# One fused attention and mixture-of-experts kernel: longer blocks of score and value matmuls, earlier q, k and v loads

## The chip, the cores and the metric

The kernel runs on one core of a Trainium2 chip. The metric is the device time of one execution in microseconds (us), lower is better. Three timed runs of the kernel before gave 984.13, 987.03 and 989.49 us; their median is 987.03 us. One more execution was taken with the hardware profiler: 983.65 us. In the instruction lists PE is TensorE's matmul stream, PEld its weight loads, DVE VectorE, ACT ScalarE, POOL GpSimd and SP SyncE, which issues most of the DMA transfers.

## What is computed

Attention with a sigmoid in place of a softmax, an expert layer with a capacity per expert, and a dense two-layer network, all in float32:

```
q, k, v: (4, 12, 448, 64)
scores = q @ k.T / 8 - log(448);  attn = sigmoid(scores);  x = attn @ v     -> (1792, 768)
logits = x @ w_gate (768, 8): tokens go to experts in the order of all logits, 224 per expert
out[mask_e] = relu(x[mask_e] @ w1[e] (768, 1024)) @ w2[e] (1024, 768)
h = relu(out @ w_in (768, 2048));  result = (s * h * h + b) @ w_out (2048, 768)
```

## The kernel before

The order of the instructions on each engine is the order of the source: nothing is rescheduled. The buffers of a tile pool are reused in turn, and an instruction that takes a buffer again waits for the last reader of its earlier content.

**Attention.** Heads are handled in 24 head pairs, i = 6 b + p (batch b of 4, pair p of 6). The q and k of a pair lie transposed as 128 x 448: head 0 in partitions 0 to 63, head 1 in 64 to 127. A score chunk c (112 of the 448 keys, both heads) is two calls of `T.matmul` with 64 rows and 112 columns of the array, one for each head (L236); a float32 call becomes two matmul instructions, so a chunk is 4 instructions and a pair has 16. A chunk fills one tile `psc` of two PSUM banks, and one ACT instruction (L237) turns it into `attn`. The value matmuls (L242) have 112 rows and 64 columns; again 16 instructions for a pair, all into one bank `pv`, which ACT copies to `xT` (L251).

`scores_av(n, i, mid)` (L222) weaves the scores of pair n = i + 1 with the values of pair i. Its loop over c2 emits two score chunks (8 instructions) and then two value chunks (8 instructions), twice. So TensorE goes score, value, score, value, 8 instructions in each block. PSUM has eight banks: two `psc` tiles (4), two `pv`, and one each for `plg` and `pt`.

**The gate.** `gate` (L253) multiplies finished pairs of xT with the gate weights, `gate_copy` has ACT copy the logits, `gate_turn` (L265) adds and transposes them, `prefs` (L278) is four DVE instructions on them. `mid(c)` (L357) places them inside the blocks: pairs 0 to 3 of a batch ahead of a score block at p = 5, pairs 4 and 5 between the two chunks of a score block at the next batch's p = 0, `gate_turn` at p = 1, and after it, at the end of that iteration, `prefs`. In the last batch `bracket` follows in three stages at p = 2, 3, 4 (DVE; PE L296 and DVE; PE L302 and DVE), and the gate of pairs 0 to 4, its copy and `gate_turn` stand around the two value blocks of the last pair. `gate_last` (L273) adds pair 5.

**Loads and conversions.** In iteration i SP issues `load_v(i + 2)` (4 buffers) and `load_qk(i + 3)` (4 buffers), 224 KB for each of v, k and q. The same SP queue carries `cv_in`, a load of 768 KB of 64-bit weights, and `cv_out`, a store of 384 KB: `convert` (L148) turns float64 into float32 bit patterns with four DVE instructions (L156 to L159), 1 or 2 conversions per iteration (`CONV`), 32 in all. The next `cv_in` waits until a conversion has read its buffer, and everything behind it in SP's queue waits with it. In the last iterations `w_dma`, `w_high` (ACT) and `w_low` (POOL) prepare the first expert weights.

After attention come the routing (rows of xT to DRAM, ten auction steps among PE, DVE and ACT), a gather, and the experts with the dense network.

Of the kernel before, what the change touches and what calls it, by code (L numbers as in the profile page):

```python
# [8 lines left out]
F32 = mybir.dt.float32  # L9
# [15 lines left out]
CP = 112  # L25
# [37 lines left out]
def tile_kernel(ctx, tc, qT, kT, v, wg, w1, w2, wi, wo, s2, b2, cst, out):  # L63
# [56 lines left out]
    qk = att.enter_context(tc.tile_pool(name="qk", bufs=4))  # L120
    vp = att.enter_context(tc.tile_pool(name="vp", bufs=2))
    at = att.enter_context(tc.tile_pool(name="at", bufs=2))
    ps_s = att.enter_context(tc.tile_pool(name="ps_s", bufs=2, space=PSUM))
    ps_v = att.enter_context(tc.tile_pool(name="ps_v", bufs=2, space=PSUM))
# [84 lines left out]
    def load_v(i):  # L209
        b, p = pairs[i]  # L210
        vt[i] = vp.tile([CP, NC, 128], F32, name="vt", bufs=4)
        nc.sync.dma_start(vt[i], v[b, p])
# [9 lines left out]
    def scores_av(n, i, mid):  # L222
        if n is not None:
            rq, rk = raw_qk.pop(n)
            attn[n] = at.tile([CP, 2, NC, S], F32, name="attn")
        if i is not None:
            a = attn.pop(i)
            pv = ps_v.tile([128, 512], F32, name="pv")
        for c2 in range(0, NC, 2):
            for c in (c2, c2 + 1):  # L230
                mid(c)
                if n is not None:
                    p = ps_s.tile([CP, 2, 512], F32, name="psc")
                    for j in range(2):
                        me = slice(j * D, (j + 1) * D)
                        T.matmul(p[:, j, :S], rk[me, c * CP:(c + 1) * CP], rq[me], start=True, stop=True)  # L236
                    A.activation(attn[n][:, :, c, :], p[:, :, :S], AF.Sigmoid, bias=nls[:CP],  # L237
                                 scale=1.0 / math.sqrt(D))
            for c in (c2, c2 + 1):
                if i is not None:  # L240
                    for j in range(2):
                        T.matmul(pv[j * 64:(j + 1) * 64, :S], vt[i][:, c, j * D:(j + 1) * D], a[:, j, c, :],  # L242
                                 start=(c == 0), stop=(c == NC - 1))
        if i is not None:
            b, p = pairs[i]
            xt = xT[:, p, b * S:(b + 1) * S]
            if i == len(pairs) - 1:
                A.copy(xt[:, :2 * CP], pv[:, :2 * CP])
                A.copy(xt[:, 2 * CP:], pv[:, 2 * CP:S])
            else:  # L250
                A.copy(xt, pv[:, :S])  # L251

    def gate(b, p0, p1, last):  # L253
        if p0 == 0:
            plg[b] = ps_l.tile([128, 512], F32, name="plg")
# [9 lines left out]
    def gate_turn(b, stop):  # L265
        lg = lgs.pop(b)
        pt = ps_l.tile([128, 512], F32, name="pt")
# [21 lines left out]
    def bracket(stage):  # L289
# [4 lines left out]
        elif stage == 1:  # L294
            pm = ps_l.tile([128, 512], F32, name="plg")
# [4 lines left out]
        else:  # L300
            pr = ps_l.tile([128, 512], F32, name="plg")
# [31 lines left out]
    cv_in()  # L333
    cv_in()
    cv_in()
    scores_av(0, None, lambda c: None)
# [14 lines left out]
    for i in range(N):  # L351
        b, p = pairs[i]
        if i + 2 < N:
            load_v(i + 2)
        if i + 3 < N:
            load_qk(i + 3)
        def mid(c):  # L357
            if b == B - 1 and p == 5:
                if c == 0:
                    gate(b, 0, 5, 5)  # L360
                elif c == 2:
                    gate_copy(b)
                elif c == 3:
                    gate_turn(b, False)
            elif p == 5 and c == 0:
                gate(b, 0, 4, 6)
            elif p == 0 and b and c == 1:
                gate(b - 1, 4, 6, 6)
            elif p == 0 and b and c == 3:
                gate_copy(b - 1)  # L370
            elif p == 1 and b and c == 0:
                gate_turn(b - 1, True)

        scores_av(i + 1 if i + 1 < N else None, i, mid)
        if p == 1 and b:
            prefs(b - 1)
# [442 lines left out]
```

## Time and profile before

| what | value |
|---|---|
| profiled execution | 983.65 us, its span 981.8 us |
| median of three timed runs | 987.03 us |
| PE busy | 938.5 us (96%) |
| DVE, ACT, POOL busy | 592.1, 449.7, 241.5 us |
| mean granted TensorE clock | 0.981 of full |
| PE matmul groups L236 and L242 | 86.1 and 82.8 us |
| DMA moved | 173.07 MB, mean 176 GB/s |

The span is counted from the first to the last instruction; 1.85 us of the profiled time lie around it. A merged row of the timeline gives the start, the time from the first start to the last end, engine, line, operation, the tile written and read, the shapes (rows*columns of the array, then the moving operand), the number of instructions, and in brackets the engine's idle time before it with what ended it. Matmul ends overlap the next start, so the pace of TensorE is read from differences of starts.

### The profile page before, as it was taken

What the parts mean: (1) busy time and instruction counts of PE and PEld (TensorE: products, weight loads), DVE (VectorE), ACT (ScalarE), POOL (GpSimd) and SP (SyncE); (2) the same over time, 40 slices, a digit from 0 to 9 for tenths busy, and PEclk for the clock granted to TensorE, in tenths of its full rate; (3) what the DMA queues carried; (4) which work ended last, traced back from release to release, by engine and by line L of the source; (5) the groups of instructions that cost most, each with busy time, mean ns of one, the idle gap of its engine ahead of it and who ended that gap; (6) DMA issues with size and microseconds to landing.
All of it is one profiled execution on the core that took longest, in us unless ns stands there. A gap on an engine that the chain in (4) does not pass through costs nothing.

```text
span 981.8 us, 13971 instructions
## 1 busy us (share of the span) xinstructions
PE 938.5 (96%) x5181; PEld 774.8 (79%) x5181; DVE 592.1 (60%) x984; ACT 449.7 (46%) x787; POOL 241.5 (25%) x183
## 2 busy tenths in 40 slices
PE   9999999768999999999999999999999999999997
PEld 3333333447889999988999999889999988899997
DVE  3655635774788970287777323877773288677320
ACT  5666657564654332366533223664332366533220
POOL 1000001225556565455200003551000164200001
PEclk9999999778999999999999999999999999999999
DMA  9999996373664344467443433664434476443321
GB/s 301 369 310 361 351 352 219 114 223 106 206 202 136 113 133 125 144 208 236 126 132 111 127 97 120 221 220 144 124 115 138 125 228 206 126 128 113 113 65 65
DMA packets 68455, 173.07 MB, mean 176 GB/s; under 512 B 7968, under 2 KB 24864, under 8 KB 68384
## 3 DMA queue, kind: packets, MB, share of 16 engines
q1 hardware_dynamic: 64256, 160.22, 50.8%
q0 software_dynamic: 2272, 11.01, 3.2%
q10 hardware_dynamic: 1856, 0.92, 0.3%
q8 instruction: 42, 0.69, 0.3%
q14 instruction: 29, 0.24, 0.1%
HBM read 148.52 MB, written 23.59 MB: 175 GB/s over the span
## 4 chain that ended last, share of the span: by engine, by line
PE 72%; DVE 16%; ACT 5%; issue 3%; DMA 2%; POOL 1%; POOLq 0%; ACTq 0%; SPq 0%; DVEq 0%
PE acc L690 8%; PE acc L691 8%; PE acc L692 8%; PE psc L236 8%; PE acc L741 8%; PE acc L742 8%; PE acc L743 8%; PE pv L242 8%; DVE u L652 6%; DVE wl L197 5%; PE acc L641 4%; ACT wh L186 2%; PE acc L642 2%; DVE tt L646 2%; DVE y L655 2%
## 5 line engine op out<-in xcount | busy, mean ns | idle before, releaser
L197 POOL TENSOR_TENSOR wl<-raw,wh 128x768 fp32r<-128x768 f32 (+1 forms) x89 | 196.5, 2215 | 422.2 <-ACT wh L186 404.5
L186 ACT CAST wh<-raw 128x768 fp32r<-128x768 f32 (+1 forms) x240 | 209.2, 879 | 160.2 <-PE acc L743 137.0
L197 DVE TENSOR_TENSOR wl<-raw,wh 128x768 fp32r<-128x768 f32 (+1 forms) x151 | 168.2, 1118 | 99.3 <-ACT wh L186 99.3
L741 PE MATMUL acc<-wh,gt 128*128 128x384 f32 x448 | 149.9, 335 | 0.0
L742 PE MATMUL acc<-wl,gt 128*128 128x384 f32 x448 | 149.7, 334 | 0.0
L743 PE MATMUL acc<-wh,gt 128*128 128x384 f32 x448 | 149.6, 334 | 0.0
L690 PE MATMUL acc<-y,wh 128*128 128x448 f32 x384 | 141.2, 368 | 0.0
L691 PE MATMUL acc<-y,wh 128*128 128x448 f32 x384 | 140.4, 366 | 0.0
L692 PE MATMUL acc<-y,wl 128*128 128x448 f32 x384 | 140.3, 365 | 0.0
L641 PE MATMUL acc<-u,wh 128*128 128x448 f32 x384 | 126.6, 384 | 14.2 <-DVE u L652 14.1
L641 PE MATMUL acc<-x,wh 128*128 128x448 f32 x384 | 124.2, 379 | 0.0
L237 ACT ACTIVATE attn<-psc,nls 112x896 f32<-112x896 f32 x96 | 92.1, 1005 | 54.3 <-PE psc L236 54.3
L642 PE MATMUL acc<-x,wl 128*128 128x224 f32 x384 | 102.3, 266 | 2.5 <-DVE wl L197 1.7
L642 PE MATMUL acc<-u,wl 128*128 128x224 f32 x384 | 102.9, 268 | 1.3 <-DVE wl L197 1.3
L714 ACT ACTIVATE r<-acc 128x448 f32<-128x448 f32 x64 | 34.9, 545 | 149.6 <-PE acc L692 149.6
L641 PEld LDWEIGHTS acc<-u,wh 128*128 128x128 f32 x384 | 72.8, 190 | 26.0 <-DVE u L652 20.8
L236 PE MATMUL psc<-rq,rk 64*112 64x448 f32 x384 | 86.1, 564 | 0.6 <-ACT attn L237 0.6
L742 PEld LDWEIGHTS acc<-wl,gt 128*128 128x128 f32 x448 | 84.1, 188 | 0.0
L741 PEld LDWEIGHTS acc<-wh,gt 128*128 128x128 f32 x448 | 84.1, 188 | 0.0
L743 PEld LDWEIGHTS acc<-wh,gt 128*128 128x128 f32 x448 | 84.1, 188 | 0.0
L242 PE MATMUL pv<-attn,vt 112*64 112x448 f32 x384 | 82.8, 552 | 0.0
L652 DVE SCALAR_TENSOR_TENSOR u<-tt,u 128x224 fp32r<-128x224 f32 x64 | 65.2, 1019 | 20.9 <-ACT u L651 19.1
(206 smaller groups left out, 1189.2 us busy)
## 6 DMA issues: line engine op xcount, KB each, us to landing
raw<-nw SPq DMA_DIRECT2D x128, 384.0 KB
raw<-in_w_dram SPq DMA_DIRECT2D x64, 384.0 KB
raw<-in_w_dram SPq DMA_DIRECT2D x48, 512.0 KB
craw<-in_wi_dram SPq DMA_DIRECT2D x16, 768.0 KB
nw<-co SPq DMA_DIRECT2D x32, 384.0 KB
craw<-in_wo_dram SPq DMA_DIRECT2D x16, 768.0 KB
rk<-in_kT_dram SPq DMA_DIRECT2D x24, 224.0 KB
rq<-in_qT_dram SPq DMA_DIRECT2D x24, 224.0 KB
```

Of the source, the lines that this page charges most:

```text
L186: A.copy(h[:, :k], raws[i][:, :k])
L197: eng.tensor_sub(lo[:, :k], r[:, :k], h[:, :k].bitcast(F32))
L236: T.matmul(p[:, j, :S], rk[me, c * CP:(c + 1) * CP], rq[me], start=True, stop=True)
L242: T.matmul(pv[j * 64:(j + 1) * 64, :S], vt[i][:, c, j * D:(j + 1) * D], a[:, j, c, :], start=(c == 0), stop=(c == NC - 1))
L641: T.matmul(p[:, :2 * CAP], wh[:, k], src[:, k].rearrange("p a s -> p (a s)"), start=(k == 0), stop=False)
L642: T.matmul(p[:, :CAP], wl[:, k], src[:, k, 0], start=False, stop=(k == n - 1))
L690: T.matmul(p, wh, src[:, k, 0], start=first, stop=False)
L691: T.matmul(p, wh, src[:, k, 1], start=False, stop=False)
L692: T.matmul(p, wl, src[:, k, 0], start=False, stop=last)
L741: T.matmul(ps[t][:, :DH], hi, wh[:, cols], start=(f == 0), stop=False)
L742: T.matmul(ps[t][:, :DH], hi, wl[:, cols], start=False, stop=False)
L743: T.matmul(ps[t][:, :DH], lo, wh[:, cols], start=False, stop=(f == KG - 1))
```

## The change

The weaving function is split in two. `scores(n, c0, c1)` emits score chunks c0 to c1 of pair n, `values(i)` all value matmuls of pair i and its copy. An iteration is now `values(i)` (16 instructions), `scores(i + 1, 2, NC)` and `scores(i + 2, 0, 2)` (16 together). Ahead of the loop all scores of pair 0 and half of those of pair 1 are made. `psc` gets three tiles of two banks, `pv` one bank, and the gate's tiles share one bank, `small`. The q and k of pair i + 4 (5 buffers) and then the v of pair i + 3 (5 buffers) are issued at the head of iteration i; pair 3's q and k and pair 2's v go ahead of the second `cv_in`. The gate's steps stand at the ends of iterations: pairs 0 to 3 (0 to 4 in the last batch) after p = 4, pairs 4 and 5 and the copy after p = 5, `gate_turn` and `prefs` after the next batch's p = 0, the stages of `bracket` after p = 1, 2, 3, and the last `gate_turn` after the loop.

```diff
@@ -117,11 +117,11 @@
     cgp = early.enter_context(tc.tile_pool(name="cgp", bufs=1))
 
     att = ExitStack()
-    qk = att.enter_context(tc.tile_pool(name="qk", bufs=4))
+    qk = att.enter_context(tc.tile_pool(name="qk", bufs=5))
     vp = att.enter_context(tc.tile_pool(name="vp", bufs=2))
     at = att.enter_context(tc.tile_pool(name="at", bufs=2))
-    ps_s = att.enter_context(tc.tile_pool(name="ps_s", bufs=2, space=PSUM))
-    ps_v = att.enter_context(tc.tile_pool(name="ps_v", bufs=2, space=PSUM))
+    ps_s = att.enter_context(tc.tile_pool(name="ps_s", bufs=3, space=PSUM))
+    ps_v = att.enter_context(tc.tile_pool(name="ps_v", bufs=1, space=PSUM))
     ps_l = att.enter_context(tc.tile_pool(name="ps_l", bufs=1, space=PSUM))
 
 
@@ -208,7 +208,7 @@
 
     def load_v(i):
         b, p = pairs[i]
-        vt[i] = vp.tile([CP, NC, 128], F32, name="vt", bufs=4)
+        vt[i] = vp.tile([CP, NC, 128], F32, name="vt", bufs=5)
         nc.sync.dma_start(vt[i], v[b, p])
 
     def load_qk(i):
@@ -219,40 +219,39 @@
         nc.sync.dma_start(rq, qT[b, p])
         raw_qk[i] = (rq, rk)
 
-    def scores_av(n, i, mid):
-        if n is not None:
-            rq, rk = raw_qk.pop(n)
+    def scores(n, c0, c1):
+        if n >= len(pairs):
+            return
+        if c0 == 0:
             attn[n] = at.tile([CP, 2, NC, S], F32, name="attn")
-        if i is not None:
-            a = attn.pop(i)
-            pv = ps_v.tile([128, 512], F32, name="pv")
-        for c2 in range(0, NC, 2):
-            for c in (c2, c2 + 1):
-                mid(c)
-                if n is not None:
-                    p = ps_s.tile([CP, 2, 512], F32, name="psc")
-                    for j in range(2):
-                        me = slice(j * D, (j + 1) * D)
-                        T.matmul(p[:, j, :S], rk[me, c * CP:(c + 1) * CP], rq[me], start=True, stop=True)
-                    A.activation(attn[n][:, :, c, :], p[:, :, :S], AF.Sigmoid, bias=nls[:CP],
-                                 scale=1.0 / math.sqrt(D))
-            for c in (c2, c2 + 1):
-                if i is not None:
-                    for j in range(2):
-                        T.matmul(pv[j * 64:(j + 1) * 64, :S], vt[i][:, c, j * D:(j + 1) * D], a[:, j, c, :],
-                                 start=(c == 0), stop=(c == NC - 1))
-        if i is not None:
-            b, p = pairs[i]
-            xt = xT[:, p, b * S:(b + 1) * S]
-            if i == len(pairs) - 1:
-                A.copy(xt[:, :2 * CP], pv[:, :2 * CP])
-                A.copy(xt[:, 2 * CP:], pv[:, 2 * CP:S])
-            else:
-                A.copy(xt, pv[:, :S])
+        rq, rk = raw_qk[n]
+        for c in range(c0, c1):
+            p = ps_s.tile([CP, 2, 512], F32, name="psc")
+            for j in range(2):
+                me = slice(j * D, (j + 1) * D)
+                T.matmul(p[:, j, :S], rk[me, c * CP:(c + 1) * CP], rq[me], start=True, stop=True)
+            A.activation(attn[n][:, :, c, :], p[:, :, :S], AF.Sigmoid, bias=nls[:CP], scale=1.0 / math.sqrt(D))
+        if c1 == NC:
+            raw_qk.pop(n)
+
+    def values(i):
+        a, v = attn.pop(i), vt.pop(i)
+        pv = ps_v.tile([128, 512], F32, name="pv")
+        for c in range(NC):
+            for j in range(2):
+                T.matmul(pv[j * 64:(j + 1) * 64, :S], v[:, c, j * D:(j + 1) * D], a[:, j, c, :],
+                         start=(c == 0), stop=(c == NC - 1))
+        b, p = pairs[i]
+        xt = xT[:, p, b * S:(b + 1) * S]
+        if i == len(pairs) - 1:
+            A.copy(xt[:, :2 * CP], pv[:, :2 * CP])
+            A.copy(xt[:, 2 * CP:], pv[:, 2 * CP:S])
+        else:
+            A.copy(xt, pv[:, :S])
 
     def gate(b, p0, p1, last):
         if p0 == 0:
-            plg[b] = ps_l.tile([128, 512], F32, name="plg")
+            plg[b] = ps_l.tile([128, 512], F32, name="small")
         for p in range(p0, p1):
             i = p % 4
             T.matmul(plg[b][i * 32:(i + 1) * 32, :S], wgs[:, p], xT[:, p, b * S:(b + 1) * S],
@@ -264,7 +263,7 @@
 
     def gate_turn(b, stop):
         lg = lgs.pop(b)
-        pt = ps_l.tile([128, 512], F32, name="pt")
+        pt = ps_l.tile([128, 512], F32, name="small")
         pts[b] = pt[:CP, :NC * E].rearrange("p (c e) -> p c e", e=E)
         for c in range(NC):
             T.matmul(pts[b][:, c], lg[:, c * CP:(c + 1) * CP], ct[:, C_SEL:C_SEL + E], start=(c == 0),
@@ -292,13 +291,13 @@
             V.tensor_reduce(mm[:CP, 0:1], lv, axis=AX.X, op=ALU.max)
             V.tensor_reduce(mm[:CP, 1:2], lv, axis=AX.X, op=ALU.min, negate=True)
         elif stage == 1:
-            pm = ps_l.tile([128, 512], F32, name="plg")
+            pm = ps_l.tile([128, 512], F32, name="small")
             T.transpose(pm[:2, :CP], mm[:CP], ident[:CP, :CP])
             m2 = ep.tile([2, 1], F32, name="m2")
             V.tensor_reduce(m2, pm[:2, :CP], axis=AX.X, op=ALU.max)
             V.tensor_scalar(dg, ident[:2, :2], m2, None, op0=ALU.mult)
         else:
-            pr = ps_l.tile([128, 512], F32, name="plg")
+            pr = ps_l.tile([128, 512], F32, name="small")
             T.matmul(pr[:, :2], on[:2], dg, start=True, stop=True)
             V.tensor_copy(mm, pr[:, :2])
             lb = ep.tile([128, 1], BF16, name="lb")
@@ -331,9 +330,12 @@
     load_v(1)
     load_qk(2)
     cv_in()
+    load_qk(3)
+    load_v(2)
     cv_in()
     cv_in()
-    scores_av(0, None, lambda c: None)
+    scores(0, 0, NC)
+    scores(1, 0, 2)
     nc.sync.dma_start(sb2[:, 0:1], s2.partition_broadcast(128))
     nc.sync.dma_start(sb2[:, 1:2], b2.partition_broadcast(128))
     G.memset(on, 1.0)
@@ -350,32 +352,25 @@
     N = len(pairs)
     for i in range(N):
         b, p = pairs[i]
-        if i + 2 < N:
-            load_v(i + 2)
+        if i + 4 < N:
+            load_qk(i + 4)
         if i + 3 < N:
-            load_qk(i + 3)
-        def mid(c):
-            if b == B - 1 and p == 5:
-                if c == 0:
-                    gate(b, 0, 5, 5)
-                elif c == 2:
-                    gate_copy(b)
-                elif c == 3:
-                    gate_turn(b, False)
-            elif p == 5 and c == 0:
-                gate(b, 0, 4, 6)
-            elif p == 0 and b and c == 1:
-                gate(b - 1, 4, 6, 6)
-            elif p == 0 and b and c == 3:
-                gate_copy(b - 1)
-            elif p == 1 and b and c == 0:
-                gate_turn(b - 1, True)
-
-        scores_av(i + 1 if i + 1 < N else None, i, mid)
-        if p == 1 and b:
+            load_v(i + 3)
+        values(i)
+        scores(i + 1, 2, NC)
+        scores(i + 2, 0, 2)
+        if p == 0 and b:
+            gate_turn(b - 1, True)
             prefs(b - 1)
-        if b == B - 1 and 2 <= p <= 4:
-            bracket(p - 2)
+        elif p == 4:
+            gate(b, 0, 4 if b < B - 1 else 5, 6 if b < B - 1 else 5)
+            if b == B - 1:
+                gate_copy(b)
+        elif p == 5 and b < B - 1:
+            gate(b, 4, 6, 6)
+            gate_copy(b)
+        if b == B - 1 and 1 <= p <= 3:
+            bracket(p - 1)
         if N - 6 <= i < N - 2:
             w_dma()
         if i >= N - 4:
@@ -384,6 +379,7 @@
         if i < N - 1:
             for _ in range(CONV[i]):
                 convert()
+    gate_turn(B - 1, False)
     gate_last(B - 1)
     prefs(B - 1)
     cv_out(0)
```

## Rows read from the trace of the kernel before

**Rows 1.** Windows: busy us (instructions) by engine, granted clock, DMA share, GB/s.

```profile
0.00:172.00 172.00, 170.24 (x820) 57.84 (x822) 92.26 (x143) 107.30 (x125) 7.19 (x17) 1.00 0.94 323
...
181.00:230.00 49.00, 32.50 (x201) 24.84 (x201) 30.04 (x215) 27.63 (x93) 11.90 (x23) 0.70 0.56 160
```

**Rows 2.** Timeline, PE, five score and five value blocks, first and last.

```profile
59.73 1.76 PE L236 MATMUL psc<-rq,rk 64*112 64x448 f32 x8
61.42 1.72 PE L242 MATMUL pv<-attn,vt 112*64 112x448 f32 x8
...
76.46 1.76 PE L236 MATMUL psc<-rq,rk 64*112 64x448 f32 x8
```

**Rows 3.** Timeline, PEld, weight loads inside one score and one value block.

```profile
60.20 0.18 PEld L236 LDWEIGHTS psc<-rq,rk 64*112 64x112 f32 x2 [0.20 <-issue]
60.58 0.18 PEld L236 LDWEIGHTS psc<-rq,rk 64*112 64x112 f32 x2 [0.20 <-issue]
...
61.85 0.14 PEld L242 LDWEIGHTS pv<-attn,vt 112*64 112x64 f32 x2 [0.23 <-issue]
62.23 0.14 PEld L242 LDWEIGHTS pv<-attn,vt 112*64 112x64 f32 x2 [0.23 <-issue]
```

**Rows 4.** Timeline, ACT, the two sigmoids of the block at 59.73.

```profile
60.85 1.91 ACT L237 ACTIVATE attn<-psc,nls 112x896 f32<-112x896 f32 x2 [1.35 <-PE psc L236]
```

**Rows 5.** Timeline, PE, a gate in the middle of a score block.

```profile
94.07 1.01 PE L236 MATMUL psc<-rq,rk 64*112 64x448 f32 x4
95.01 0.94 PE L258 MATMUL plg<-xT,wgs 128*32 128x448 f32 x4
95.89 1.01 PE L236 MATMUL psc<-rq,rk 64*112 64x448 f32 x4
96.83 1.72 PE L242 MATMUL pv<-attn,vt 112*64 112x448 f32 x8
```

**Rows 6.** Timeline, PE, scores of pairs 0 and 1, first values.

```profile
7.81 1.91 PE L236 MATMUL psc<-rq,rk 64*112 64x448 f32 x8 [0.36 <-ACT attn L237]
9.92 1.91 PE L236 MATMUL psc<-rq,rk 64*112 64x448 f32 x8 [0.21 <-ACT attn L237]
11.76 1.72 PE L242 MATMUL pv<-attn,vt 112*64 112x448 f32 x8
```

**Rows 7.** Timeline, PE, the last pairs of attention.

```profile
172.63 0.38 PE L302 MATMUL plg<-dg,on 2*128 2x2 f32 x2
173.78 1.69 PE L258 MATMUL plg<-xT,wgs 128*32 128x448 f32 x10 [0.77 <-DVE mm L303]
...
177.05 0.95 PE L270 MATMUL pt<-ct,lg 128*112 128x8 f32 x8
177.93 1.72 PE L242 MATMUL pv<-attn,vt 112*64 112x448 f32 x8
180.10 0.95 PE L275 MATMUL pt<-wgs,xT 128*112 128x8 f32 x8 [0.45 <-ACT xT L248]
```

**Rows 8.** Timeline, DVE, the last conversions and the last preferences.

```profile
168.39 2.46 DVE L159 CUSTOM_DVE_ANT_0 co<-co,cb__1306 128x1536 uint16<-128x1536 uint16 x1
...
176.16 0.55 DVE L156 TENSOR_SCALAR co<-craw 128x768 int32<-128x768 int32 x1
...
178.08 0.96 DVE L159 CUSTOM_DVE_ANT_0 co<-co,cb__1363 128x1536 uint16<-128x1536 uint16 x1
181.09 0.19 DVE L279 COPY L<-pt 112x32 f32<-112x32 f32 x1 [2.05 <-PE pt L275]
```

**Rows 9.** Timeline, POOL, beside them.

```profile
167.21 2.82 POOL L197 TENSOR_TENSOR wl<-raw,wh 128x768 fp32r<-128x768 f32 x1 [4.87 <-ACT wh L186]
```

**Rows 10.** Windows, as in Rows 1, a stretch without a hold of SP.

```profile
110.00:140.00 30.00, 30.00 (x150) 9.59 (x148) 16.80 (x24) 18.50 (x23) 0.00 (x0) 1.00 1.03 367
```

**Rows 11.** Timeline, SP and PE, issue and first use of pair 11's k.

```profile
66.68 0.46 SPq L217 DMA_DIRECT2D rk<-in_kT_dram  x1
...
79.80 1.39 PE L236 MATMUL psc<-rq,rk 64*112 64x448 f32 x6
```

## The prediction

> **What bounds the kernel now.** I read the windows first: in the first 172 us TensorE is busy for 170.24, at a granted clock of 1.00 of full (its 2.4 GHz level), while DVE and ACT are busy for 92 and 107 [rows 1]. So attention is bound by TensorE alone, and a microsecond saved there ends the stage a microsecond earlier. The DMA engines are busy for 94% of the same stretch [rows 1]; they are the next limit and have to be looked at. The routing behind it, 181 to 230 us, is a chain of short steps at a mean granted clock of 0.70 [rows 1] that the change doesn't touch.
>
> Then the timeline of TensorE. Five score and five value blocks of 8 follow each other from 59.73 to 76.46: 16.73 / 5 = 3.346 us for one of each, the score block 1.69 of it and the value block 1.66 [rows 2]. Inside a block the weight loads show the pace: the two matmuls of both heads run side by side, and the next two come 0.38 us later, in score blocks (60.20, 60.58) as in value blocks (61.85, 62.23) [rows 3]. Four such steps of 0.375 are 1.50 us. The rest, 0.19 for a score block and 0.155 for a value block, is paid once per block: when TensorE turns from 64 rows and 112 columns to 112 rows and 64 columns, or back, the next kind starts only after the last one has run out, and its first loads are not hidden. That is what longer blocks can save.
>
> **The change part by part, on TensorE.**
>
> *Blocks of 16.* From the first value matmul on, the kernel before runs 48 value blocks (two for each of 24 pairs) and 45 score blocks; the one after 24 and 23. Removed: 24 x 0.155 + 22 x 0.19 = 7.9 us. The matmuls stay the same in number. A block of 16 should take 8 x 0.375 + 0.19 = 3.19 us (scores) and 3.155 (values), an iteration 6.35 in place of 6.69.
>
> *The gate.* Pairs 4 and 5 of a batch stand in the middle of a score block: from 94.07 to 96.83 are 2.76 us, where the block alone takes 1.69, so 1.07 [rows 5]. At a block's edge the gate's own step is 0.88 (95.01 to 95.89), as it replaces one turn by two. Three batches x 0.19 = 0.6 us. The other gate steps stood at edges and stand at edges again: nothing.
>
> *The last batch.* The gate at 173.78 waited 0.77 us for DVE, which had just been asked to copy the result of the matmul at 172.63 [rows 7]. After, a whole iteration lies between them: 0.8 gained. `gate_turn` (177.05 to 177.93, 0.88) leaves the gap between the last two value blocks and goes behind them, where `gate_last` waits for the copies of xT anyway: the last block would have ended at 177.93 + 1.65 = 179.58 and `gate_last` began at 180.10 [rows 7], 0.52 later; now it begins 0.88 later. 0.88 - 0.36 = 0.5 gained.
>
> *Ahead of the loop.* Before, the third and the fifth score chunk waited 0.36 and 0.21 us for a sigmoid to free one of two psc tiles, and the first values began at 11.76 [rows 6]. With three tiles the sixth chunk waits for the third sigmoid. The first ended at 7.8 (it released the chunk at 7.81), two sigmoids take 1.91 us [rows 4], so the third ends at 9.7; the chunk takes 0.94 [rows 5], and the values begin at about 10.7: 1.0 gained, between 0 (ACT as before) and 1.2.
>
> Sum: 7.9 + 0.6 + 0.8 + 0.5 + 1.0 = 10.8 us.
>
> **What can wait in the new order.** An ACT iteration is four sigmoids (2 x 1.91) and a copy, 4.4 us of 6.35, so ACT keeps up. `pv` with one bank: its copy starts when the values are done, a score block of 3.19 us lies ahead of the next values; hidden. The sigmoids of pair i + 1's last two chunks are made in the first half of the score block and needed after it; hidden. One edge is sharp: the fourth chunk of a score block takes the psc tile of the first. Its sigmoid begins 1.12 us after the block (59.73 to 60.85) and ends about 1.0 later [rows 2, 4], at 2.1; the chunk is due at 0.46 + 5 x 0.375 = 2.34 (the first step is 0.46 long, 59.73 to 60.20 [rows 2, 3]), but its weights are loaded one step earlier, at 1.96. No such wait is in the trace. It costs nothing if the loads hide behind the step before, and at most 0.1 us x 22 if they don't, with nothing to gain from it: 0 to 2.2. I take 0.4, nearer the end at nothing, since the sigmoid ends before the matmul is due. Everything behind it on TensorE waits as well.
>
> The shared bank `small` is taken in turn by steps that are an iteration apart: nothing.
>
> **DMA and SP.** On SP's queue the loads of q and k pass those of v, and both come an iteration earlier in the order; the first conversions' loads come three transfers (0.7 MB, 2 us at 367 GB/s [rows 10]) later, and a conversion is not waited for. `prefs` now stands an iteration earlier in DVE's order while its matmul comes at nearly the same point of TensorE's, so DVE stands still longer there, and `cv_in` and the q, k and v loads behind it on SP wait with it. After the first hold, which ended with the gate's turn just ahead of 59.73, the k of pair 11 was issued at 66.68 and used at 79.80, 13.1 us later [rows 2, 11]. Now one conversion, some 4 us with its load, lies between the end of the hold and the next pair's q and k, and their use is two iterations and 4.75 us (a value block and half a score block) behind it: 2 x 6.35 + 4.75 - 4 = 13.4 us. The busiest batch carries 9 conversions (1.18 MB each) and six pairs (0.69 MB each), 14.7 MB in 6 x 6.35 + 3 x 0.88 (gate) = 40.7 us, 362 GB/s; 367 were moved from 110 to 140 us [rows 10]. Balanced, with the 13 us as a cushion: I cost it at nothing, and below as a rival.
>
> **DVE's last work.** Behind the matmul of the third `bracket` stage DVE now has three conversions ahead of the last `prefs` (it had one). Before: 172.63 to 176.16 for the stage, then 2.88 for a conversion (176.16 to 179.04), and then 2.05 us of waiting for TensorE [rows 7, 8]. After, DVE is done 3.53 + 3 x 2.88 = 12.2 us behind that matmul; TensorE needs 0.38 + 3.155 + 1.69 + 1.62 (173.78 to 175.40) + 3.155 + 0.88 + 0.99 (180.10 to 181.09 [rows 7, 8]) = 11.9. So this is a draw: the cover of 2 us is gone. One conversion lost 1.5 us (2.46 in place of 0.96 for its last step, 168.39) while POOL's subtraction ran from 167.21 to 170.03 [rows 8, 9]. With none such, DVE is early: 0; with two, late by 0.3 + 3.0 = 3.3. POOL has two subtractions in that stretch and may be the one that waits; I take 0.6, nearer the draw that the durations give. The Trainium skill ("SBUF — State Buffer", Who interferes with whom) says that a DVE instruction with two SBUF inputs and a reading GpSimd instruction shut each other out, and whoever issues first holds the port for its whole length; by that every meeting that POOL begins costs up to the 1.8 us of its subtraction, and two would make 3.6. The trace agrees in kind (1.5 us), and both lengthened here.
>
> Net: 10.8 - 0.4 - 0.6 = 9.8 us. The profiled execution took 983.65 us (981.8 of it span), so its counterpart is 973.9. The median of the runs shown, 987.03, lies 3.4 above it and the lowest at 984.13; from the median, **977.2 us**.
>
> **Rivals.**
> 1. *The end of attention is given to DVE, and the fourth chunk waits.* For it: the draw above. Against: each part has a way to cost nothing. With 3.3 and 2.2 the gain is 5.3 to 7: 981.
> 2. *The cost is paid per chunk, not per turn.* If a semaphore wait at each chunk made the first step long, blocks of 16 would save nothing: 10.8 - 7.9 = 2.9, less 1.0 as above: 985. Against it: a block holds two chunks, and the step between them is 0.38 like the others [rows 3].
> 3. *Loads of the value matmuls are not hidden in a long block.* Here a load of 0.14 us would be added to every step, and value blocks would keep their 0.155 per 8: 3.7 us less, 981. Rows 3 speak against it: 0.38 from step to step with the loads included. The Trainium skill ("TensorE: Matmul & The Clock Gate", What overlaps and what doesn't) says that weight loads overlap running matmuls only when their row groups differ, and the value matmuls use the same rows; the trace doesn't bear that out.
> 4. *Slower: the loads starve TensorE.* If the longer hold empties the DMA queues and the rate after it is not 367 but under 295 GB/s, a batch's 14.7 MB take 50 us in place of 40.7, more than the 6 or so of the cushion that a load's own 7 us leave. TensorE then stands still more than 3.3 us in each of three batches; at 5 us each the net is -15 + 10: 992 to 994. For it: 94% busy DMA and a mean of 323 GB/s [rows 1]. Against: that mean includes the holds, and without them 367 were reached [rows 10].
>
> **How the numbers follow.** Forecast 0.62, rival 1 0.17, rival 2 0.08, rival 3 0.06, rival 4 0.07. The forecast's own bounds (no cost at all; both costs at their ends; no gain ahead of the loop) are 976.2 and 983; a median of three runs that scatter from 984 to 989 moves each end, 4 us below and 1 above: 972 to 984. That holds rivals 1 and 3 too. About 0.5% (4.9 us) is what a measurement of this kernel can tell from no change: faster means below 982.1, slower above 992. The forecast and most of rivals 1 and 3 are faster: 0.81; rival 2 and the rest of those 0.13; rival 4 0.06.
>
> **What would show it.** In the profile after: PE blocks of 16, with 3.19 and 3.15 us from start to start, 48 blocks in all; steps of 0.38 throughout, and a longer seventh step in score blocks where the psc wait bites; the first values at 10.7; the last gate without a wait; `gate_last` near 169.5 in place of 180.1; the last L279 on DVE waiting for TensorE (draw won) or starting at once behind a conversion (lost). From there on both traces should run alike. I am wrong if the blocks of 16 take over 3.3 us, if TensorE waits for q, k or v in the middle of a batch, or if the routing takes back what attention gives.

## The result and the profile after

The kernel after took a median of 978.67 us (8 runs, 974.86 to 981.26), the kernel before 987.38 on the same chip (8 runs, 984.13 to 989.49): a ratio of 0.9915, 95% interval 0.9894 to 0.9935, so 8.7 us less. Forecast were 977.2 us and 9.8 us less. The profiled execution after took 977.76 us, its span 976.0.

The timeline of PE in the middle of attention answers to [rows 2]:

```profile
57.99 3.23 PE L242 MATMUL pv<-attn,vt 112*64 112x448 f32 x16
61.15 3.26 PE L232 MATMUL psc<-rq,rk 64*112 64x448 f32 x16
64.34 3.23 PE L242 MATMUL pv<-attn,vt 112*64 112x448 f32 x16
67.50 3.26 PE L232 MATMUL psc<-rq,rk 64*112 64x448 f32 x16
```

From start to start a value block of 16 takes 3.16 us (57.99 to 61.15), a score block 3.19 (61.15 to 64.34), the next ones alike, and no bracket tells of a wait. (From the first values on there are 24 value blocks, 22 score blocks of 16 and one of 8, so 47 and not the 48 of the forecast.) So neither the fourth chunk's tile nor a load stopped TensorE. The windows answer to [rows 1] and [rows 10] (columns as there):

```profile
0.00:160.00 160.00, 158.81 (x806) 61.38 (x808) 89.01 (x141) 101.87 (x122) 4.50 (x16) 1.00 0.95 340
...
110.00:140.00 30.00, 30.00 (x162) 11.45 (x160) 15.90 (x24) 20.18 (x25) 0.00 (x0) 1.00 1.03 392
...
176.00:208.00 32.00, 25.85 (x132) 21.91 (x132) 20.71 (x178) 24.19 (x82) 7.20 (x18) 0.50 0.71 208
```

Attention is still bound by TensorE, and the DMA engines moved 392 GB/s where they had moved 367. The last line is the routing: its granted clock was 0.50 throughout (the 1.2 GHz level), where [rows 1] had 0.70. That is no accident of this one execution: all 8 runs after had a mean granted clock of 0.967 to 0.972 over their whole span (the profiled one, which is one of them, 0.970), while of the 62 runs of the kernel before that stand beside the experiments 17 were at 0.972 or below and the others at up to 0.984. The end of attention, PE and then DVE and POOL, answers to [rows 7], [rows 8] and [rows 9]:

```profile
158.75 0.38 PE L301 MATMUL small<-dg,on 2*128 2x2 f32 x2
163.91 1.69 PE L257 MATMUL small<-xT,wgs 128*32 128x448 f32 x10
165.53 3.23 PE L242 MATMUL pv<-attn,vt 112*64 112x448 f32 x16
168.68 0.95 PE L269 MATMUL small<-ct,lg 128*112 128x8 f32 x8
169.49 0.93 PE L274 MATMUL small<-wgs,xT 128*112 128x8 f32 x8
...
174.02 0.32 PE L419 MATMUL pl<-ident,L 112*128 112x112 f32 x1 [3.12 <-DVE L L278]
```

```profile
161.59 0.97 DVE L158 SCALAR_TENSOR_TENSOR co<-craw,co 128x768 int32<-128x768 int32 x1
162.59 2.45 DVE L159 CUSTOM_DVE_ANT_0 co<-co,cb__1327 128x1536 uint16<-128x1536 uint16 x1
...
166.88 0.96 DVE L159 CUSTOM_DVE_ANT_0 co<-co,cb__1334 128x1536 uint16<-128x1536 uint16 x1
167.76 2.17 DVE L156 TENSOR_SCALAR co<-craw 128x768 int32<-128x768 int32 x1
...
170.32 2.56 DVE L158 SCALAR_TENSOR_TENSOR co<-craw,co 128x768 int32<-128x768 int32 x1
172.91 0.96 DVE L159 CUSTOM_DVE_ANT_0 co<-co,cb__1371 128x1536 uint16<-128x1536 uint16 x1
173.78 0.18 DVE L278 COPY L<-small 112x32 f32<-112x32 f32 x1
174.00 0.43 DVE L282 TENSOR_TENSOR ge<-L 112x256 f32<-112x256 f32 x1
```

```profile
161.11 3.12 POOL L197 TENSOR_TENSOR wl<-raw,wh 128x768 fp32r<-128x768 f32 x1 [4.59 <-ACT wh L186]
166.97 2.54 POOL L197 TENSOR_TENSOR wl<-raw,wh 128x768 fp32r<-128x768 f32 x1 [2.75 <-ACT wh L186]
170.20 1.85 POOL L197 TENSOR_TENSOR wl<-raw,wh 128x768 fp32r<-128x768 f32 x1 [0.69 <-ACT wh L186]
```

The gate at 163.91 and `gate_last` at 169.49 start without a wait. But DVE makes the last copy into L at 173.78, directly behind a conversion, and not at 170.5 when `gate_last` is done: 3.3 us late. It still had that conversion to do, and two of its steps ran beside POOL's subtractions and took longer: 2.17 us in place of 0.55, and 2.56 in place of 0.95. A step two conversions earlier had done the same (2.45 in place of 0.96, at 162.59).

The two profiles by stage, in us:

| stage | before | after | gain |
|---|---|---|---|
| start to the first values | 11.76 | 10.88 | 0.88 |
| first values to `gate_last` | 168.34 | 158.61 | 9.73 |
| `gate_last` to the auction's first matmul | 4.77 | 6.62 | -1.85 |
| ten auction steps | 30.59 | 32.45 | -1.86 |
| rest of the routing | 14.23 | 14.29 | -0.06 |
| first expert matmul to the end | 752.09 | 753.12 | -1.03 |
| span | 981.78 | 975.97 | 5.81 |

The profiles differ by 5.8 us, the medians by 8.7, since the profiled execution before was among the shortest of its kind; experiment e10 shows a part of what sets it apart. The last but one row is not read: from the first expert matmul to the end the fourteen profiled executions take 752.1 to 755.8 us, without a change there.

### The profile page after: what moved, and what is told of

It is laid out like the page before. It is cut to its first block, busy times and chain, and to the rows that moved or that the text cites. A ratio compares the mean times of both kernels' runs of the same rounds, so it can differ in the third digit from the quotient of the medians.

```text
span 976.0 us, 13964 instructions
## 1 busy us (share of the span) xinstructions
PE 936.0 (96%) x5181; PEld 785.5 (80%) x5181; DVE 597.3 (61%) x984; ACT 446.4 (46%) x787; POOL 242.7 (25%) x183
## 4 chain that ended last, share of the span: by engine, by line
PE 75%; DVE 16%; ACT 4%; issue 2%; DMA 1%; POOL 0%; POOLq 0%; ACTq 0%; SPq 0%; DVEq 0%
PE acc L686 8%; PE acc L688 8%; PE acc L687 8%; PE acc L737 8%; PE acc L739 8%; PE acc L738 8%; PE psc L232 8%; PE pv L242 7%; DVE u L648 6%; PE acc L637 6%; DVE wl L197 5%; PE acc L638 3%; ACT wh L186 2%; DVE tt L642 2%; PE px L404 2%
## 5 line engine op out<-in xcount | busy, mean ns | idle before, releaser
L233 ACT ACTIVATE attn<-psc,nls 112x896 f32<-112x896 f32 x96 | 88.9, 1008 | 14.2 <-PE psc L232 14.2
L232 PE MATMUL psc<-rq,rk 64*112 64x448 f32 x384 | 79.3, 553 | 0.0
L242 PE MATMUL pv<-attn,vt 112*64 112x448 f32 x384 | 77.5, 545 | 0.0
L637 PEld LDWEIGHTS acc<-x,wh 128*128 128x128 f32 x384 | 72.7, 189 | 5.7 <-DVE x L632 0.5
```

Of the source, the lines that this page charges most:

```text
L242: T.matmul(pv[j * 64:(j + 1) * 64, :S], v[:, c, j * D:(j + 1) * D], a[:, j, c, :], start=(c == 0), stop=(c == NC - 1))
L637: T.matmul(p[:, :2 * CAP], wh[:, k], src[:, k].rearrange("p a s -> p (a s)"), start=(k == 0), stop=False)
```

## The experiments

The theory: TensorE pays a fixed price at each turn between the two kinds of matmul, and half of the turns are gone; DVE's last conversions give about 2 us of it back. The rivals are those of the prediction. Each kernel ran beside the kernel before on its chip. Edits are to the kernel after, except in e5 and e10.

**e1, blocks of 8 again, all else as after** (`values` now takes a range of chunks; only its calls are shown).

```diff
-        values(i)
-        scores(i + 1, 2, NC)
+        values(i, 0, 2)
+        scores(i + 1, 2, NC)
+        values(i, 2, NC)
         scores(i + 2, 0, 2)
```

> The kernel after, but its value block is cut in two and woven into the two halves of its score block, so blocks are 8 matmuls again; buffers, loads, gate places and conversions stay as after. If a turn between the two shapes costs 0.155 and 0.19 us (the forecast's step), 24 value and 22 score turns come back: blocks of 1.65 and 1.69 us, gate_last at 169.5 + 7.9 = 177.4 us and the whole 7 to 8 us slower than after (986). If the cost is paid per chunk or per wait (rival), gate_last stays at 169.5 and the time at 978.7.

985.95 us, ratio 0.9988 (0.9967 to 1.0009): the gain is gone. Timeline, PE:

```profile
65.04 1.76 PE L232 MATMUL psc<-rq,rk 64*112 64x448 f32 x8
66.73 1.72 PE L245 MATMUL pv<-attn,vt 112*64 112x448 f32 x8
68.38 1.76 PE L232 MATMUL psc<-rq,rk 64*112 64x448 f32 x8
```

The blocks take the 1.69 and 1.65 us of [rows 2] again, and the stage from the first values to `gate_last` takes 166.20 us, 7.59 more than after. Counted in the trace, from the first values to `gate_last` TensorE now runs 105 blocks and gate steps in place of 60 (the last pair's values stayed one block), so 45 turns were added: 0.169 us each. The early loads are still in this kernel, and its time is that of the kernel before: without the longer blocks they bring no gain.

**e5, the kernel before with blocks of 4.** It holds each chunk's work fixed and doubles the turns.

```diff
-        for c2 in range(0, NC, 2):
-            for c in (c2, c2 + 1):
+        for c2 in range(0, NC):
+            for c in (c2,):
```

> The kernel before with blocks of 4 matmuls (one score chunk, one value chunk, and so on). If each turn has its fixed price, 46 value and 45 score turns are added: 46 x 0.155 + 45 x 0.19 = 15.7 us, blocks of 0.94 and 0.905 us, gate_last at 195.8 in place of 180.1 and the whole near 1002.5. If the price is per chunk or per wait, nothing changes (987).

1001.04 us, ratio 1.0137 (1.0110 to 1.0164). Timeline, PE:

```profile
63.56 1.01 PE L236 MATMUL psc<-rq,rk 64*112 64x448 f32 x4
64.50 0.97 PE L242 MATMUL pv<-attn,vt 112*64 112x448 f32 x4
65.40 1.01 PE L236 MATMUL psc<-rq,rk 64*112 64x448 f32 x4
```

A pair of blocks of 4 takes 1.84 us, two of them 3.68, against 3.346 for a pair of 8. The stage grew by 15.24 us over the kernel before, and there are 198 blocks and gate steps in place of 109: 89 more turns, 0.171 us each. With e1 this is a price per turn that holds for 4, 8 and 16; rival 2 falls.

**e2, two psc tiles.**

```diff
-    ps_s = ... (name="ps_s", bufs=3, space=PSUM)
-    ps_v = ... (name="ps_v", bufs=1, space=PSUM)
+    ps_s = ... (name="ps_s", bufs=2, space=PSUM)
+    ps_v = ... (name="ps_v", bufs=2, space=PSUM)
```

> The kernel after with the PSUM split of before: two psc tiles and two pv in place of three and one. If the third psc tile is what carries blocks of 16, the third chunk of a score block waits for the first sigmoid (due at 1.59 us, free at about 2.2) and the fourth for the second (due 2.9, free 3.1): 0.8 us in each of 22 blocks and 1 ahead of the loop, gate_last near 188 us in place of 169.5, the whole at 995, slower than before. If the tiles don't matter (rival: ACT is far from busy, 4.4 of 6.35 us), gate_last stays at 169.5.

995.46 us, ratio 1.0092 (1.0059 to 1.0124): slower than before. Timeline, PE:

```profile
67.64 1.76 PE L232 MATMUL psc<-rq,rk 64*112 64x448 f32 x8
69.76 1.90 PE L232 MATMUL psc<-rq,rk 64*112 64x448 f32 x8 [0.36 <-ACT attn L233]
71.59 3.23 PE L242 MATMUL pv<-attn,vt 112*64 112x448 f32 x16
```

Here the third chunk takes the tile of the first, and the score block takes 3.95 us (67.64 to 71.59), 0.76 more; 22 times that is 16.7, and the stage grew by 16.73. The third tile is a condition of the gain, and with it the wait is nil.

**e4, the loads no earlier than before.**

```diff
-        if i + 4 < N:
-            load_qk(i + 4)
         if i + 3 < N:
-            load_v(i + 3)
+            load_qk(i + 3)
+        if i + 2 < N:
+            load_v(i + 2)
```

(and pair 3's q and k and pair 2's v not ahead of the loop)

> The kernel after with the load distances of before: q and k three pairs ahead, v two, and nothing but pairs 0 to 2 (v: 0 and 1) ahead of the loop. In the trace after, the shortest time from issue to use is 10.5 us (q of pair 17); a pair less is 4.2, and a load takes about 5 us there. If the loads are a cushion that is nearly used up behind SP's holds, TensorE now waits 1 to 2 us for q, k at two or three places: gate_last 1 to 5 us later and the time at 979 to 984. If the loads were never near the path, gate_last stays at 169.5.

986.12 us (979.36 to 989.90, so the loss is not in every run), ratio 0.9993 (0.9968 to 1.0019): by the median far more than was expected. Timeline, PE, then SP's issues, then windows (columns as in [rows 1]):

```profile
108.29 1.76 PE L232 MATMUL psc<-rq,rk 64*112 64x448 f32 x8
...
112.62 2.51 PE L232 MATMUL psc<-rq,rk 64*112 64x448 f32 x8 [2.57 <-DMA rq<-in_qT_dram]
115.06 4.13 PE L242 MATMUL pv<-attn,vt 112*64 112x448 f32 x16
...
166.58 5.67 PE L242 MATMUL pv<-attn,vt 112*64 112x448 f32 x16
```

```profile
104.85 0.33 SPq L140 DMA_DIRECT2D craw<-in_wo_dram  x1
...
105.74 0.44 SPq L219 DMA_DIRECT2D rq<-in_qT_dram  x1
```

```profile
113.60:116.80 3.20, 3.20 (x11) 0.86 (x10) 2.77 (x4) 2.01 (x2) 0.00 (x0) 0.50 1.03 363
164.80:171.40 6.60, 6.60 (x20) 2.21 (x18) 4.51 (x12) 2.73 (x3) 1.80 (x1) 0.50 0.76 258
```

The q, issued at 105.74 behind a conversion's 768 KB after SP's hold, was used at 112.62, 6.9 us later. Five blocks are longer than in the kernel after (by 1.29, 3.57, 0.90, 2.81 and 2.44 us), 11.0 us together; the stage grew by 11.2. Three of them wait for a q, but the waits are only half of it: 1.03, 2.57 and 1.90, so 5.5 us. The two value blocks, at 115.06 and 166.58, wait for nothing; they lie in stretches in which the granted clock was 0.50, behind the waits of 2.57 and 1.90, and a part of the score matmuls that follow those waits lies in them too. So a late load costs twice here, by the wait and by the clock behind it. The expectation had 5 us for a load; the three that TensorE waited for took 6.9 to 9.4 from issue to use. So the gain needs the earlier loads as well; in the kernel after the shortest time from issue to use is 10.5 us (q of pair 17), and rival 4 was held off by 1 to 3.5 us, not by 13.

**e3, the last conversion moved out of attention, behind the auction.**

```diff
-            for _ in range(CONV[i]):
+            for _ in range(CONV[i] - (i == N - 2)):
...
     places(lambda: rows(len(turns)))
+    convert()
+    cv_out(0)
```

> The kernel after, but the last of the 32 conversions is made behind the placing of the tokens, where DVE waits for the gather, instead of ahead of the last preferences. If DVE's last conversions hold up the routing (rival 1 of the prediction), the last L copy on DVE starts at 170.4 us in place of 173.78 and the whole gets up to 3.4 us faster (975.5). If the routing is bound elsewhere, or the gather is delayed by the conversion, the copy moves but the first expert matmul doesn't, and the time stays at 978.7.

975.87 us, ratio 0.9891 (0.9863 to 0.9919). Timelines, DVE and PE:

```profile
169.52 0.19 DVE L278 COPY L<-small 112x32 f32<-112x32 f32 x1 [0.86 <-PE small L274]
...
217.77 2.48 PE L631 MATMUL acc<-ident,xr 128*128 128x128 f32 x12 [4.22 <-DVEq L585]
```

L now waits for TensorE, 0.97 us after `gate_last` starts, and the auction begins 2.2 us earlier. But the gathered rows are used 8.44 us after TensorE's matmuls of zeros behind the auction begin, in place of 6.51: DVE does the conversion ahead of a branch that stands behind the gather, and PE waits for DVE's sequencer there. In the two profiled executions these nearly cancel; the auction was shorter by 1.8 us as well (30.64 in place of 32.45), with 10 us of it at the full clock, so the lower median is not the earlier L alone.

**e6, the two POOL subtractions moved away, the conversion left.**

```diff
         if i >= N - 4:
             w_high()
-            w_low(G)
+            if i < N - 2:
+                w_low(G)
...
+            if fill and it in (1, 2):
+                w_low(G)
```

> The kernel after, but POOL makes its last two subtractions (those at 166.97 and 170.20) in the auction's second and third step instead of beside DVE's last conversion. If the two meetings are what made that conversion 6.0 us long in place of 2.9, the last L copy on DVE starts at 170.7 in place of 173.78; if three conversions are simply too many, it stays above 172. The auction pays for it: two subtractions of 1.8 us lie in POOL's part of its chain, so the whole may come out at 976 to 981.

977.22 us (2 runs), ratio 0.9905 (0.9873 to 0.9936). Timeline, DVE:

```profile
166.71 0.55 DVE L156 TENSOR_SCALAR co<-craw 128x768 int32<-128x768 int32 x1
...
167.64 0.95 DVE L158 SCALAR_TENSOR_TENSOR co<-craw,co 128x768 int32<-128x768 int32 x1
168.63 0.96 DVE L159 CUSTOM_DVE_ANT_0 co<-co,cb__1369 128x1536 uint16<-128x1536 uint16 x1
169.51 0.18 DVE L278 COPY L<-small 112x32 f32<-112x32 f32 x1
```

Without POOL the same conversion takes 2.9 us in place of 6.0, and L comes 1.1 us behind `gate_last`, again directly behind the conversion but only 0.1 late. So the lateness was the meetings with POOL and not the conversion; without these two the draw of the prediction is a draw (the earlier meeting, of the subtraction at 160.05, is still there). The whole gains little, as the subtractions now lengthen the auction (35.15 us).

**e7, the conversion behind POOL's gathers** (as e3, with a one-element copy from POOL ahead of it). Is the loss in e3 the branch or the gather?

```diff
+    G.memset(spacer, 0.0)
+    sp2 = rp.tile([1, 1], F32, name="sp2")
+    V.tensor_copy(sp2, spacer)
+    convert()
+    cv_out(0)
```

> Like the run with the last conversion behind the placing, but DVE begins it only when POOL has issued both gathers. There the time from the clock-keeping matmuls to the first expert matmul rose from 8.6 to 10.9 us. If the conversion held up POOL's gathers, it is 8.6 to 8.9 again and the whole about 974; if the store or the later branch is to blame, it stays at 10.9 and the whole at 976.

979.95 us, ratio 0.9915 (0.9885 to 0.9945). Timeline, PE:

```profile
222.11 1.19 PE L634 MATMUL acc<-ident,xr 128*128 128x128 f32 x5 [6.25 <-DVEq L583]
```

From the matmuls of zeros to the first expert matmul are 12.6 us, more than either reading of the expectation. The conversion began behind both gathers and cost more than in e3. DVE ended it at 218.2, and the rows are used 3.9 us later, with DVE's sequencer, at the branch, named as what PE waited for. What holds the branch is not settled. The conversion's store stands ahead of it too, on SP: SP passes the branch at 220.30, behind DVE (218.31), and in e3 at 214.63, behind DVE (212.75), while in the kernel after SP is the first there. No run leaves the store out and keeps the conversion.

**e8, one conversion from iteration 21 to 19.**

```diff
-CONV = [1, 1, 2, 1, 2] * 4 + [1, 2, 1]
+CONV = [1, 1, 2, 1, 2] * 3 + [1, 1, 2, 1, 3] + [1, 1, 1]
```

> The kernel after with one conversion moved from iteration 21 to iteration 19, where DVE then stands idle for 2.9 us ahead of the second bracket stage. Two conversions are left behind the third stage. The last L copy then starts at 170.4 to 171 in place of 173.78, the first choice at 4.5 to 5 us behind gate_last in place of 6.6, and nothing is given back at the gather: 2 us faster than after, 976.5. If the loads of the weights don't come that fast, the second bracket stage is late and TensorE waits: no gain or a loss.

977.99 us, ratio 0.9914 (0.9896 to 0.9932). L is made 0.97 us behind `gate_last`, and the auction's first matmul comes 4.49 behind it in place of 6.62: 2.1 us gained and none given back at the gather. The median isn't measurably below that of the kernel after.

**e9, e10 and e11: the clock of the routing.** Matmuls of zeros into a spare tile that nobody reads, 8 behind the first transpose and 2 to 4 in each auction step; e9 is e8 with them, e10 the kernel before, e11 the kernel after.

```diff
     A.copy(LT, pl)
+    spare = ps_r.tile([128, 512], F32, name="pi")[:CP]
+    keep_clock(8, spare)
...
+            if fill:
+                keep_clock(8 - 2 * ROWS[it], spare)
             V.scalar_tensor_tensor(LM, pv, -BIG, LT, ...)
```

> The kernel with the tail moved to iteration 19, and matmuls of zeros that nobody reads in the routing: 8 between the two first transposes and 4 (beside 8 transposes) or 2 (beside 12) in each auction step. In the profiles so far the ten steps took 30.6 us where the granted clock was at its full level for 10 to 14 us in their middle, and 32.45 where it stayed at half for 44 us. If the half clock makes the steps with 12 transposes long (2.60 in place of 1.86 us), the fillers keep it at full, the steps take 30.6 us or less in every run, and the whole comes to 975 to 976. If the clock falls all the same, a step with 4 fillers at half clock takes 3.4 us of TensorE where 1.86 are free, and the auction grows by up to 15 us: 985 to 992.

> The kernel before with the same fillers and nothing else. Its profiled execution had the full level in the middle of the auction (30.6 us), its median run is 3.4 us longer than that execution. If the difference between its runs comes from the routing's clock, its runs now come near 983 to 984 and scatter less; if not, the median stays at 987 or grows with the fillers.

> The kernel after with the same fillers in the routing and nothing else, to be set beside the kernel before with fillers (982.7). With the routing's clock at full in both, the difference left is what attention gives: 9.7 us between the first value matmul and gate_last (168.34 to 158.61), about 1 ahead of the loop, less 2.2 at the last preferences: 8.5 us, so 974 to 974.5. If attention's gain is given back elsewhere, the difference is under 6 us.

e9: 975.80 us, ratio 0.9909 (0.9888 to 0.9930). e10: 982.74 us against 985.93, ratio 0.9967 (0.9953 to 0.9981). e11: 979.09 us, ratio 0.9933 (0.9908 to 0.9957). Windows in the routing, before and e10:

```profile
185.00:215.00 30.00, 20.94 (x132) 17.04 (x132) 20.53 (x179) 24.10 (x83) 7.20 (x18) 0.73 0.76 222
```

```profile
185.00:215.00 30.00, 23.17 (x167) 16.78 (x166) 21.25 (x183) 24.55 (x83) 7.21 (x18) 1.00 0.76 222
```

With the fillers the granted clock stays at 1.00, and the ten steps take 29.60 us in all three. Without them they take 32.45 where the clock is at half throughout (after), and 30.59 where 13.6 us of them ran at full (before). The e10 runs lie within 2.6 us (981.12 to 983.72), those of the kernel before beside them within 6.0 (982.75 to 988.76), and the median is 3.2 lower: which of its steps run at half is a large part of what scatters there. It isn't all: the ten steps differ by up to 2.9 us (29.60 to 32.45), and the runs of e9 and e11, with the steps at full, still spread over 6.6 us. e11 missed its 974: L was late there too, and behind PE's wait of 3.26 us the granted clock went from 1.00 (172 to 174 us) to 0.50 (175 to 177; timeline, PE):

```profile
174.19 0.32 PE L419 MATMUL pl<-ident,L 112*128 112x112 f32 x1 [3.26 <-DVE L L278]
174.34 3.47 PE L318 MATMUL pi<-zero 128*112 128x512 bf16 x8
...
178.51 0.21 PE L430 MATMUL pa<-aw,cb 128*128 128x112 bf16 x1 [0.51 <-DVE aw L428]
```

The eight fillers took 3.47 us at half, ahead of the transpose that the chain needs, and the auction began 9.01 us behind `gate_last` in place of 6.62. So e11 is 3.7 us below e10 where 8.5 were expected, and by the criterion of its expectation a part of attention's gain is given back: 2.4 us of the nearly 5 that are missing are these fillers, the rest is open. (The two ran on different chips.)

**e12, the kernel of e9 once more, beside e11.**

> The kernel with fillers and the earlier conversion a second time, on the chip of the run beside it: the tail alone is then worth 2.2 us (6.6 in place of 4.4 from gate_last to the first choice), so 972 if the other is 974.2. In the first set of runs its profiled execution took 970.9 and its timed ones 974.4 to 977.6; if that spread has its cause in the first values' start (9.5 there, 10.9 after), a second profile may show a later start.

973.52 us (971.67 to 977.73), ratio 0.9876 (0.9847 to 0.9904) to 986.38. Timeline, PE:

```profile
170.34 0.29 PE L419 MATMUL pl<-ident,L 112*128 112x112 f32 x1
170.47 1.89 PE L318 MATMUL pi<-zero 128*112 128x512 bf16 x8
...
173.45 0.21 PE L430 MATMUL pa<-aw,cb 128*128 128x112 bf16 x1 [0.51 <-DVE aw L428]
```

With L on time the same fillers take 1.89 us, and the auction begins 4.36 behind `gate_last`. That is 4.65 of the 5.6 us between the medians of e11 and e12. This version has the lowest median of all, below both kernels; but it was not timed beside the kernel after, and the intervals of its two studies (0.9909 and 0.9876) overlap that of 0.9915, so how much it is better than that is open. What spreads its runs, with the clock at full, is open too.

## Why the prediction came out

**Blocks of 16: right.** 3.19 and 3.155 were forecast, 3.19 and 3.16 measured; e1 puts the turns back and loses 7.59 of the 7.9 us, and e5 doubles those of the kernel before. The Trainium skill ("TensorEngine Tiling (Array Packing)", Key Properties) says that changing the tiling mode drains TensorE; the trace agrees, at 0.169 to 0.171 us a turn here (0.155 and 0.19 were forecast for the two kinds). Rivals 2 and 3 fall: value blocks of 16 are as fast per step as those of 8.

**The gate and the last batch: right.** With the blocks, 7.9 + 0.6 + 0.8 + 0.5 = 9.8 us were forecast and 9.73 measured; in e1, which has the new places but blocks of 8, the stage is 2.14 us shorter than before, where 0.6 + 0.8 + 0.5 = 1.9 were forecast. `gate_last` starts at 169.49, forecast near 169.5.

**Ahead of the loop: right in kind.** 1.0 forecast, 0.88 measured; over all traces the first values came between 9.5 and 10.9 us with three psc tiles (ten traces) and between 10.3 and 12.1 with two (four), so the direction holds and the size is no firmer than that.

**The fourth chunk's wait: 0.4 taken, 0 measured.** The lower bound held.

**Loads: right, for a cushion that was too large.** Nothing was lost, and 392 GB/s were reached; but e4 shows that the earlier order was needed for the gain, and that the margin is 1 to 3.5 us.

**DVE's last work: mis-sized.** It was called a draw and cost 0.6 us; L was 3.3 late, the upper end. 1.45 came back, as `ge`, which met a subtraction in the kernel before, no longer does (0.43 in place of 1.87), so 1.85 was lost. Timelines of the kernel before, DVE and then POOL:

```profile
174.65 1.27 DVE L311 COPY dv<-mm 128x8 f32<-128x8 f32 x1
...
181.32 1.87 DVE L283 TENSOR_TENSOR ge<-L 112x256 f32<-112x256 f32 x1
```

```profile
174.09 1.81 POOL L197 TENSOR_TENSOR wl<-raw,wh 128x768 fp32r<-128x768 f32 x1 [4.05 <-ACT wh L186]
```

The step that failed is "POOL has two subtractions in that stretch and may be the one that waits". That POOL waits did not spare DVE. Between the third `bracket` matmul and L three subtractions met DVE and not two. They took 3.12, 2.54 and 1.85 us where one by itself takes 1.81, so POOL waited 1.3 and 0.7 at the first two, and DVE lost 1.49, 1.62 and 1.61 all the same, 4.7 together. That L came no later than the upper end for two is partly luck, as the 3.53 us taken for the `bracket` stage had waits of its own in them: DVE was still at a conversion, and its copy at 174.65 met a subtraction (1.27 us, after the change 0.16). After, the stage took 1.90 (158.75 to 160.65), 1.6 less. Who waits first doesn't follow from the order of the starts: POOL's 2.54 begins inside DVE's addition (to 167.84) and ends ahead of DVE's next step, which begins at 167.76 and is held up, but POOL's 3.12 begins at 161.11, ahead of the DVE step at 161.59, and that step runs undisturbed (0.97). So what the Trainium skill ("SBUF — State Buffer", Who interferes with whom) says fits in that the two shut each other out, and its estimate in the prediction, up to 3.6 for two meetings, was the better one for the last conversion, 3.23 measured; that whoever issues first goes first is not what the rows at 161.11 show.

**Not foreseen: the routing's clock.** "From there on both traces should run alike" failed by 1.86 us in the auction, which ran at half throughout in this execution. e10 shows that this belongs to the routing, and the mean clocks given with the result that it comes and goes in the kernel before, but whether the late L makes the half clock likelier was not settled. For it: the three profiled executions with L late and no fillers (after, e1, e2) ran the auction at half throughout, and so, by their mean clock, did all 8 runs after. Against it: of those with L on time the kernel before, e3 and e8 had stretches at full, but e4, e5, e6 and e7 had none.

The sum came out since attention, the large part, was read from rows that repeat more than forty times, and the mis-sized part had its bounds. The stages of the two profiled executions differ by less than the medians do (5.8 against 8.7 us), so that the medians come within 1.5 us of the forecast also rests on how the runs of the kernel before scatter.

## What to carry to other kernels

Where matmuls of two array shapes alternate, read the price of a turn from the steps inside a block and the length of a block, and count turns; then see whether buffers and loads reach far enough for the longer blocks, as the lack of either took all the gain here (e2, e4). Where two engines' last instructions come out as a draw and a GpSimd instruction with SBUF operands starts in that stretch, lay the two timelines over each other and charge every meeting to DVE, here 1.1 to 1.7 us each, even where GpSimd waits too. And a saving ahead of a chain that isn't bound by TensorE can be lost in the clock: look at the granted clock there in several traces before calling it unchanged. A wait of TensorE can cost twice its length in the same way (e4).

## What the runs showed of the hardware

In the routing after, PE was busy for 25.85 of 32 us, mostly with short transposes, and yet had a granted clock of 0.50; with matmuls of zeros added to each step it stayed at 1.00 (e10). Behind a wait of 3.26 us at the end of attention the clock fell to half, and eight such matmuls took 3.47 us in place of 1.89 (e11, e12); behind waits of 2.57 and 1.90 us in attention it fell too, and a value block that waited for nothing took 5.59 us in place of 3.16 (e4). A DVE instruction with one input in SBUF (`TENSOR_SCALAR`, 0.55 us) took 2.17 beside a GpSimd subtraction, so it is held up like one with two. And with a conversion on DVE and its store on SP put ahead of a branch, TensorE waited behind it for 4.22 and 6.25 us (e3 and e7), though it takes no data from them; which of the two it waits for was not separated.
